# Adding the causal mask of a diagonal score block with VectorE instead of with a matmul, with new planner priorities

## The chip, the core and the metric

The kernel runs on one core of a Trainium2 chip. The core has a matrix engine (TensorE, called PE in the profile; its weight loads are PEld), and three other compute engines: VectorE (DVE), ScalarE (ACT) and GpSimd (POOL). SyncE (SP) issues all the transfers of this kernel. Matmul results land in PSUM, which the kernel divides into eight banks of 128 partitions by 512 fp32 columns. The metric is the device time of one execution in microseconds (us); of several executions the median counts. A separate, profiled execution gives the trace, and its span runs from the first to the last instruction.

## The reference, cut to what matters

The input x is 2048 tokens of 448 numbers. One branch (A) is attention with 16 heads of 28 numbers, in four segments of 512 tokens with a memory carried between segments; the other (B) is a feed-forward layer of width 1792 with SiLU. A learned gate mixes the two.

```python
def _A_ref(x, wq, wk, wv, wo, beta):
    # q, k, v: (x @ w), split into 16 heads of 28 and 4 segments of L = 512
    mask = (ar[:, None] < ar[None, :]) * (-1e9)          # causal, ar = arange(512)
    for s in range(4):
        logits = einsum("bhqd,bhkd->bhqk", qs, ks) * scale + mask
        p = softmax(logits, axis=-1)
        a_dot = einsum("bhqk,bhkd->bhqd", p, vs)
        a_mem = (phi(qs) @ M) / (phi(qs) . z + 1e-6)      # memory of earlier segments
        o = g * a_mem + (1 - g) * a_dot                   # g = sigmoid(beta), per head
        M, z = M + phi(ks)^T vs, z + sum(phi(ks))
    return concat(o) @ wo

b = silu(x @ w1) @ w2
g = sigmoid((x * gate_w).sum(-1, keepdims=True))
return g * _A_ref(...) + (1 - g) * b
```

The softmax needs, for each query row, the maximum of its masked scores. With large query and key weights these scores are large, and the kernel computes the true row maxima.

## The kernel before, in words

**Stages.** The first stage (`project`) loads x and the weights, projects q, k and v for the four segments, and builds the memory. After it two things run side by side: attention, and the feed-forward layer (`ffn`, `unit`) in two passes, over 10 and then 4 of its 14 blocks of 128 hidden columns. The last stage finishes the second feed-forward pass, multiplies the attention output by wo and writes the result.

**Attention by groups.** Attention runs over 16 groups, each four heads of one segment. Function `attention` calls `maxima` for its group. `maxima` loads the group's q and k into a tile named `ring` (four transfers by SP) and then walks a plan of eleven score tiles, each in one PSUM bank of the ring `sc`, which has three banks. Query block i is 128 query rows, and sees only the first 128(i+1) keys, so the tiles are: block 0 of all four heads in one bank (4 x 128 columns), block 1 of two heads per bank (2 x 256), and blocks 2 and 3 of one head per bank (384 and 512). For every tile TensorE computes the scores (line 666, function `go`), and VectorE takes the row maxima (function `red`) into the tile `mx`.

**The mask.** In blocks 1 to 3, one fused VectorE instruction per head (line 676) adds the mask tile `MK`, a 128 x 512 fp32 tile whose last 128 columns hold the causal triangle, and reduces to the maximum. In block 0 the mask comes from TensorE: line 662 multiplies the bf16 identity `identb` by the bf16 triangle `maskb` into all four heads' columns, the four score matmuls accumulate on it, and VectorE reduces once (line 671) over the four heads. The triangle in `maskb` is made once by GpSimd (line 752), from a zeroed tile that the warm-up matmuls of line 740 use first.

**What follows.** When all eleven tiles of a group are reduced, VectorE subtracts a lift (line 684), TensorE transposes the maxima (line 686), ScalarE and VectorE split them in two fp16 parts (lines 688, 690), and SP writes and reloads them as extra rows of `ring`. Then the scores are computed again, transposed (line 1222, also in the `sc` banks), exponentiated by ScalarE (line 1227), masked by GpSimd (lines 1230, 1233), rounded by ScalarE (line 1239), their rest taken by GpSimd (line 1243), and multiplied with v by TensorE (line 1256). Feed-forward products are line 561 (first layer; the same helper does q, k, v and wo) and line 1124 (second layer); their results are worked on by ScalarE (1101, 1105, 1163) and VectorE (1103, 1107).

**What sets the order.** The kernel does not write its instructions in program order. Each step is a task with an engine, an estimated duration, the tasks it needs, the buffers it takes, and a priority (a lower number goes first). The class `Sched` plays the tasks through, always starts the earliest task that can start, and among ready ones takes the lowest priority; on TensorE it adds a price (`PRICE`) for weight loads that would stand uncovered. The result is one fixed order of instructions per engine, and SP's transfers are in one queue. So a change in an estimated duration or a priority can move any instruction of any engine.

**The priorities that the diff touches.** Group t of attention has priority about 40t and head n 10n. `MAXO` is how far ahead of its group the maxima stand. `LOP` is added to the three GpSimd subtractions of a head (line 1243). `FLO` and `FHI` are the ends over which the first feed-forward pass is spread on the same scale, and the second pass and the load of wo start from `FHI`. `WBP` is the priority at which the first ten blocks of w2 are loaded and split (`wb`, lines 521 and 513). `WOP` and `WOT` are how far the wo product and the preparation of its operand (`features`, lines 572, 578, 586) stand ahead of the last additions.

Of the kernel before, what the change touches and what calls it, by code (L numbers as in the profile page):

```python
# [14 lines left out]
OP = mybir.AluOpType  # L15
# [3 lines left out]
S, D, H, DH, NSEG, L, F = 2048, 448, 16, 28, 4, 512, 1792  # L19
# [11 lines left out]
NEG = -1.0e30  # L31
# [10 lines left out]
UP = 2.0 ** 14  # L42
DOWN = 2.0 ** -24
TINY = 2.0 ** -40
WOT = 62.75
TUS = 1.6
TLAT = 4.0

# [3 lines left out]
HO = 0.09  # L52
HS = 0.14
SLACK = 0.88
LOP = 11.31
LATE = 0.08
FIRST = 120.0
WPRIO = 120.0
MAXO = 65.18
FULL = 0.111  # L60
LOCK = 0.06
RB = "cc"
# [15 lines left out]
    return o + VA + VS * k if o or k > VF else -1.0 + 0.1 * k  # L78


PRICE = 31.16
PVRUNS = [((1, 0), 1)]
PVP = 45.12
FLO = -11.7
FHI = 710.96
WOP = 118.93
SZ = 20.35
SZSTEP = 2.77
XPRIO = 74.67
WBP = -20.36  # L90
XLEAD = 146.82


# [149 lines left out]
def infini_mix(ctx: ExitStack, tc: tile.TileContext, x, wq, wk, wv, wo, beta, w1, w2, out):  # L243
    nc = tc.nc
# [39 lines left out]
    def half(cols, n=1):  # L284
        return [(0.0025 + cols * 0.000418, 0.027)] * n

    def pe(seq, fn, *deps, **k):
        t = sch.add("PE", sum(max(a[0], b[1]) for a, b in zip(seq, seq[1:])) + seq[-1][0], fn, deps, **k)
        t.lead, t.tail = seq[0][1], seq[-1][0]
        return t  # L290
# [7 lines left out]
    def dve(cols, fn, *deps, **k):  # L298
        return sch.add("DVE", 0.07 + 0.00104 * cols, fn, deps, **k)
# [4 lines left out]
    def pool(cols, fn, *deps, **k):  # L304
        return sch.add("POOL", 0.1 + 0.0019 * cols, fn, deps, **k)
# [16 lines left out]
    MK = const.tile([128, L], F32, name="mk")  # L322
    identb = const.tile([128, 128], BF, name="identb")
    maskb = const.tile([128, 128], BF, name="maskb")
# [19 lines left out]
    hs = const.tile([128, NSEG], F32, name="hs")  # L344
# [16 lines left out]
    base = ctx.enter_context(tc.tile_pool(name="base", bufs=1))  # L361
# [275 lines left out]
    AT, RS, MKS, ONE, RDONE = {}, {}, [], [], []  # L637
# [4 lines left out]
    def maxima(t, o):  # L642
        rg, mx = Buf(RG), Buf(C["mx"])
        early = o - 70
        rs = []
        for j, scr, st, lo, dup in ((0, qscr[t], QST[t], 0, 2 * DH), (1, kscr[t], KST[t], DH, 0)):
            rs.append(dma(260e3, lambda j=j, lo=lo, scr=scr: start(
                rg.v[lo:lo + 2 * DH, j], scr.rearrange("z d h n -> (z d) h n")), st, *(rs[:1] or RDONE),
                          takes=[] if rs else [rg], uses=[rg], prio=early))
            rs.append(dma(190e3, lambda j=j, dup=dup, scr=scr: start(rg.v[dup:dup + DH, j], scr[0]), st, *rs[:1],  # L650
                          uses=[rg], prio=early))
        RDONE[:] = RS[t] = rs
        reds = []
        plan = [(0, [0, 1, 2, 3]), (1, [0, 1]), (1, [2, 3])] + [(i, [h]) for h in range(4) for i in (2, 3)]
        for q, (i, hs) in enumerate(plan):
            ps = Buf(BK["sc"])
            n = 128 * (i + 1)
            p0 = o - MAXO + 40 * q / len(plan)

            def go(i=i, hs=hs, ps=ps, n=n):  # L660
                if i == 0:
                    nc.tensor.matmul(ps.v, identb, maskb[:, None, :].to_broadcast([128, 4, 128]), start=True,
                                     stop=False, skip_group_check=True)
                for j, hh in enumerate(hs):
                    u = j * n
                    nc.tensor.matmul(ps.v[:, u:u + n], rg.v[:KS, 0, hh, i * 128:(i + 1) * 128], rg.v[:KS, 1, hh, :n],  # L666
                                     start=(i > 0), stop=(i > 0 or j == 3), skip_group_check=(i == 0))

            def red(i=i, hs=hs, ps=ps, n=n):
                if i == 0:  # L670
                    nc.vector.tensor_reduce(mx.v[:, :, 0], ps.v.rearrange("p (h n) -> p h n", h=4), axis=AX.X,
                                            op=OP.max)
                    return
                for j, hh in enumerate(hs):
                    r = ps.v[:, j * n:(j + 1) * n]
                    nc.vector.tensor_tensor_reduce(r, r, MK[:, L - n:], 1.0, NEG, OP.add, OP.max,  # L676
                                                   mx.v[:, hh, i:i + 1])
            m = pe((half(512) if i == 0 else []) + half(n, len(hs)), go, *rs, *MKS, takes=[ps], uses=[rg], prio=p0)
            reds.append(dve(len(hs) * (n + 70) - 70, red, m, *reds[:1], takes=[] if reds else [mx], uses=[ps, mx],
                            prio=p0))  # L680
        pt, mh = Buf(BK["sc"]), Buf(C["mhl2"])
        p0 = o - 20
        s = t // NG
        f0 = dve(100, lambda: nc.vector.tensor_scalar(mx.v, mx.v, lift[:, s:s + 1], None, op0=OP.subtract), *reds, EREADY[s],
                 uses=[mx], prio=p0)
        f1 = pe(half(128), lambda: nc.tensor.transpose(pt.v[:16, :128], mx.v.rearrange("p h i -> p (h i)"), ident), f0,
                takes=[pt], uses=[mx], prio=p0)
        f3 = act(128, lambda: nc.scalar.activation(mh.v[:, 0], pt.v[:16, :128], AF.Copy, scale=1.0 / TALL), f1, takes=[mh],
                 uses=[pt], prio=p0)
        f4 = dve(128, lambda: nc.vector.scalar_tensor_tensor(mh.v[:, 1], pt.v[:16, :128], 1.0 / TALL, mh.v[:, 0],  # L690
                                                             op0=OP.mult, op1=OP.subtract), f3, uses=[pt, mh], prio=p0)
        d1 = dma(16e3, lambda: start(mscr[t].rearrange("z h i n -> (h i) z n"), mh.v), f4, uses=[mh], prio=p0)
        dm = dma(16e3, lambda: start(rg.v[KS:KS + 2, 0], mscr[t].rearrange("z h i n -> z h (i n)")), d1, uses=[rg],
                 prio=p0)
        return rg, rs, dm

    def project():
# [32 lines left out]
        def c1():  # L730
            for v in vtiles:
# [8 lines left out]
        t_wb = pe(half(L, WARM), lambda: [nc.tensor.matmul(  # L740
            wb.v, maskb, maskb[:, None, :].to_broadcast([128, 4, 128]), start=True, stop=True) for _ in range(WARM)],
            t_wm, takes=[wb], prio=-200)
        END1.append(t_wb)
        t_on = dve(32, lambda: nc.vector.memset(ones, -TALL), prio=-50)
        t_mb = dve(128, lambda: nc.vector.tensor_copy(identb, ident), t_id, prio=-50)
# [3 lines left out]
        t_mz = dve(L, lambda: nc.vector.memset(MK, 0.0), prio=-50)  # L749
        MKS.append(pool(128, lambda: nc.gpsimd.affine_select(MK[:, 384:], MK[:, 384:], [[-1, 128]], OP.is_ge, NEG,  # L750
                                                             base=0, channel_multiplier=1), t_mz, prio=-50))
        MKS.append(pool(128, lambda: nc.gpsimd.affine_select(maskb, maskb, [[-1, 128]], OP.is_ge, NEG, base=0,
                                                             channel_multiplier=1), t_wb, t_mb, prio=-50))
        ONE.append(dma(16e3, lambda: start(onescr.rearrange("a h (b n) -> (a h b) n", b=16), ones[:, :32]), t_on,
                       prio=50))

# [286 lines left out]
        for i, (j, src, n, how) in enumerate(pieces):  # L1043
            r, p = Buf(RAW), SZ + i * SZSTEP
# [238 lines left out]
    for t in range(NT):  # L1283
        attention(t)
    prio = spread(FLO, FHI, NSEG * len(PASSES[0]) * (11 * L + TB * 3 * D))
    ends = ffn(0, prio, part)
# [125 lines left out]
```

## Time and profile before

| what | value |
|---|---|
| median of the runs | 568.44 us (567.11 to 569.01, 3 runs) |
| profiled execution, its time | 570.06 us |
| profiled execution, its span | 568.3 us |
| granted TensorE clock, mean | 0.996 |
| PE busy | 549.6 us, 97% of the span |
| DVE busy | 421.8 us, 74% |
| ACT busy | 400.8 us, 71% |
| POOL busy | 360.0 us, 63% |

The page of the profile gives the busy time of each engine, the span in 40 slices, the chain of work that ended last, and the costliest groups of instructions. A group row reads: line, engine, operation, output from input, shape, count, then busy time, mean time of one instruction in ns, and how long the engine stood idle just before those instructions and what ended that idle time. Matmuls are pipelined: a row's mean is the time from a matmul's start to its result, while the next matmul starts earlier, so for TensorE the step from one start to the next in the timeline is what one more matmul takes. Neighbouring VectorE instructions also overlap a little. The profiled execution's time is 1.76 us longer than its span and 1.62 us longer than the median of the runs.

### The profile page before, as it was taken

The page shows a single profiled execution, that of the slowest core. Times are in us where ns is not written, and L with a number is a line of the kernel's source. Part 1 is how long each engine was busy: PE and PEld are TensorE (multiplying, and loading weights), DVE is VectorE, ACT ScalarE, POOL GpSimd, SP SyncE. Part 2 cuts the span into 40 slices and gives each one's busy share as a digit, 9 for nine tenths or more (in the row PEclk, how much of TensorE's full clock was granted, in tenths as well). Part 3 has the DMA queues.
Part 4 walks back from the last instruction along what each step waited for, and adds up shares of the span by engine and source line. Part 5 has one row for each costly group of instructions (what it writes and reads, how often), then busy time and mean ns, then how long its engine had stood idle before and what let it go on. Part 6 is the DMA issues. An engine that isn't in the chain of part 4 may idle for free.

```text
span 568.3 us, 11664 instructions
## 1 busy us (share of the span) xinstructions
PE 549.6 (97%) x4055; PEld 344.0 (61%) x4055; DVE 421.8 (74%) x1096; ACT 400.8 (71%) x695; POOL 360.0 (63%) x502
## 2 busy tenths in 40 slices
PE   8799999999989999999999999999999999999997
PEld 5588878888834455555665554555555555454544
DVE  6999889787868978598865789775888128735644
ACT  6658869675746978889887998877998887213231
POOL 5803347347220688999999988999999993122210
PEclk9999999999989999999999999999999999999999
DMA  8587856534746444422433524374400224798931
GB/s 301 175 249 225 260 150 202 159 108 143 231 147 180 132 152 153 137 72 69 114 101 100 150 78 151 101 157 125 120 14 25 84 67 122 226 232 234 238 104 66
DMA packets 80362, 83.13 MB, mean 146 GB/s; under 512 B 44296, under 2 KB 67976, under 8 KB 80304
## 3 DMA queue, kind: packets, MB, share of 16 engines
q1 hardware_dynamic: 80304, 82.39, 49.8%
q8 instruction: 32, 0.52, 0.4%
q14 instruction: 26, 0.21, 0.1%
HBM read 52.60 MB, written 26.09 MB: 138 GB/s over the span
## 4 chain that ended last, share of the span: by engine, by line
PE 66%; DVE 15%; ACT 8%; DMA 6%; issue 3%; POOL 1%; SPq 1%; DVEq 0%; ACTq 0%; POOLq 0%
PE mm L561 23%; PE mm L1124 18%; PE sc L561 9%; PE sc L1222 4%; DVE sc L676 4%; PE cc L1256 4%; PE sc L666 4%; ACT pf L1227 2%; ACT phl L1239 2%; DVE sizes L385 2%; DVE ghl L1107 1%; DMA rwo<-in_wo_dram 1%; DMA rawf<-in_x_dram 1%; DMA rawf<-in_w_dram 1%; DMA xraw<-in_x_dram 1%
## 5 line engine op out<-in xcount | busy, mean ns | idle before, releaser
L1243 POOL TENSOR_TENSOR phl<-pf,phl 128x384 f16<-128x384 f32 (+1 forms) x192 | 190.1, 1008 | 14.6 <-ACT phl L1239 14.3
L1124 PE MATMUL mm<-wb,ghl 128*128 128x448 f16 (+1 forms) x684 | 146.9, 349 | 0.3 <-DVE ghl L1107 0.3
L561 PE MATMUL mm<-xh,wa 128*128 128x512 f16 x572 | 143.7, 382 | 1.4 <-DVE ghl L1107 1.4
L676 DVE CUSTOM_DVE_ANT_0 sc<-sc,mk 128x384 f32<-128x384 f32 (+1 forms) x192 | 105.0, 570 | 30.1 <-PE sc L666 25.0
L1227 ACT ACTIVATE pf<-sc,es 128x512 f32<-128x512 f32 (+1 forms) x192 | 110.2, 621 | 17.2 <-PE sc L1222 14.1
L1124 PEld LDWEIGHTS <-ghl 128*128 128x128 f16 x684 | 65.1, 97 | 52.7 <-issue 2.1
L561 PEld LDWEIGHTS <-wa 128*128 128x128 f16 x572 | 54.5, 98 | 58.7 <-issue 6.5
L1239 ACT ACTIVATE phl<-pf 128x1280 f16<-128x1280 f32 x64 | 81.3, 1274 | 10.9 <-POOL pf L1233 10.8
L1222 PE MATMUL sc<-ring 86*128 86x512 f16 (+3 forms) x256 | 58.9, 299 | 3.4 <-DVE mx L676 1.5
L666 PE MATMUL sc<-ring 84*128 84x128 f16 (+3 forms) x256 | 57.3, 299 | 1.0 <-DVE mx L676 0.9
L1101 ACT ACTIVATE th<-mm,ths 128x512 f32<-128x512 f32 x52 | 36.1, 697 | 24.3 <-PE mm L561 24.0
L1256 PEld LDWEIGHTS <-phl 128*128 128x128 f16 x1280 | 41.7, 96 | 10.4 <-POOL phl L1243 0.6
L561 PE MATMUL mm<-xT,wqs 128*128 128x512 f32 x176 | 47.1, 404 | 0.0
L572 POOL TENSOR_TENSOR ol<-ol,ml 128x448 f32<-128x448 f32 x12 | 13.8, 1152 | 51.6 <-DMA ol<-o_scr 41.9
L561 PE MATMUL mm<-xT,wks 128*128 128x512 f32 x176 | 45.6, 397 | 0.0
L1103 DVE SCALAR_TENSOR_TENSOR mm<-th,mm 128x512 f32<-128x512 f32 x52 | 35.7, 692 | 11.8 <-ACT th L1101 11.6
L1256 PE MATMUL cc<-vg,phl 128*128 128x29 f16 (+1 forms) x1280 | 43.8, 182 | 0.1
L561 PE MATMUL sc<-wvs,xT 128*128 128x450 f32 x176 | 40.3, 375 | 1.2 <-DVE wvs L819 0.6
L1264 DVE TENSOR_REDUCE oraw<-cc 128x116 f32<-128x232 f32 x64 | 25.2, 393 | 21.5 <-PE cc L1256 21.3
L1107 DVE SCALAR_TENSOR_TENSOR ghl<-mm,ghl 128x512 f16<-128x512 f32 x52 | 35.3, 682 | 6.3 <-ACT ghl L1105 6.2
L1105 ACT ACTIVATE ghl<-mm 128x512 f16<-128x512 f32 x52 | 31.0, 604 | 12.2 <-DVE mm L1103 12.0
L1222 PEld LDWEIGHTS <-ring 86*128 86x128 f16 x256 | 24.0, 97 | 23.3 <-issue 2.9
(167 smaller groups left out, 910.4 us busy)
## 6 DMA issues: line engine op xcount, KB each, us to landing
rawf<-in_w_dram SPq DMA_DIRECT2D x26, 256.0 KB
rawf<-in_w_dram SPq DMA_DIRECT2D x28, 224.0 KB
xraw<-in_x_dram SPq DMA_DIRECT2D x16, 256.0 KB
rawf<-in_x_dram SPq DMA_DIRECT2D x16, 256.0 KB
v_scr<-vt SPq DMA_DIRECT2D x16, 232.0 KB
vg<-v_scr SPq DMA_DIRECT2D x16, 232.0 KB
q_scr<-stg SPq DMA_DIRECT2D x16, 224.0 KB
k_scr<-stg SPq DMA_DIRECT2D x16, 224.0 KB
```

What stands on the lines that cost most here:

```text
L561: nc.tensor.matmul(ps(), *p[i], start=(i == 0), stop=(i == n - 1))
L666: nc.tensor.matmul(ps.v[:, u:u + n], rg.v[:KS, 0, hh, i * 128:(i + 1) * 128], rg.v[:KS, 1, hh, :n], start=(i > 0), stop=(i > 0 or j == 3), ...
L676: nc.vector.tensor_tensor_reduce(r, r, MK[:, L - n:], 1.0, NEG, OP.add, OP.max, mx.v[:, hh, i:i + 1])
L1101: e1 = sact(L, lambda ps=ps, th=th: nc.scalar.activation(th.v, ps.v, AF.Tanh, scale=ths[:, s:s + 1]), m, takes=[th], uses=[ps], prio=p0)
L1103: e2 = dve(L, lambda ps=ps, th=th: nc.vector.scalar_tensor_tensor(ps.v, th.v, 1.0, ps.v, op0=OP.add, op1=OP.mult), e1, uses=[ps, th], prio=p0)
L1107: e4 = dve(L, lambda ps=ps, g=g: nc.vector.scalar_tensor_tensor(g.v[:, 1], ps.v, DOWN, g.v[:, 0], op0=OP.mult, op1=OP.subtract), e3, uses= ...
L1124: nc.tensor.matmul(ps.v[:, lo:hi], g.v[:, y, sl], w.v[:, z, lo:hi], start=(j == 0 and i == 0), stop=(j == len(fs) - 1 and i == 2))
L1222: nc.tensor.matmul(ps.v[:, e:e + w], rg.v[:KK, 1, hh, j * 128:(j + 1) * 128], rg.v[:KK, 0, hh, j * 128:], start=True, stop=True)
L1227: ex.append(sact(e, lambda b=b, ps=ps, pf=pf, e=e: nc.scalar.activation(pf.v[:, b, :e], ps.v[:, :e], AF.Exp, scale=es[:, s:s + 1]), m, *ex ...
L1239: hi = copy(1280, lambda hl=hl, flat=flat: nc.scalar.activation(hl.v[:, 0], flat(), AF.Copy), *mk, takes=[hl], uses=[pf], prio=p0 + 2)
L1243: low = pool(w - u, lambda hl=hl, flat=flat, u=u, w=w: nc.gpsimd.tensor_sub(hl.v[:, 1, u:w], flat()[:, u:w], hl.v[:, 0, u:w]), low, uses=[ ...
L1256: nc.tensor.matmul(p[:, i, :2 - z], hl.v[:, z, u:u + 128], vg.v[:, j, hh, :2 - z], start=(z == zs[0] and i == 0), stop=(z == zs[-1] and j ...
```

## The change

In block 0 the mask matmul goes: the four score matmuls each start and end their own sum, and VectorE adds the last 128 columns of `MK`, repeated for the four heads, to the bank in place before it reduces. `maskb` stays zero and serves only the warm-up. The planner is told 512 columns less for the TensorE task and 430 more for the VectorE task. Eight priority numbers and prices are different.

```diff
-WOT = 62.75
+WOT = 82.89
-LOP = 11.31
+LOP = 14.2
-MAXO = 65.18
+MAXO = 63.68
-PRICE = 31.16
+PRICE = 36.46
-FLO = -11.7
-FHI = 710.96
-WOP = 118.93
+FLO = -10.69
+FHI = 694.58
+WOP = 121.06
-WBP = -20.36
+WBP = -28.66
...
             def go(i=i, hs=hs, ps=ps, n=n):
-                if i == 0:
-                    nc.tensor.matmul(ps.v, identb, maskb[:, None, :].to_broadcast([128, 4, 128]), start=True,
-                                     stop=False, skip_group_check=True)
                 for j, hh in enumerate(hs):
                     u = j * n
                     nc.tensor.matmul(ps.v[:, u:u + n], rg.v[:KS, 0, hh, i * 128:(i + 1) * 128], rg.v[:KS, 1, hh, :n],
-                                     start=(i > 0), stop=(i > 0 or j == 3), skip_group_check=(i == 0))
+                                     start=True, stop=True)
 
             def red(i=i, hs=hs, ps=ps, n=n):
                 if i == 0:
+                    nc.vector.tensor_add(ps.v.rearrange("p (h n) -> p h n", h=4), ps.v.rearrange("p (h n) -> p h n", h=4),
+                                         MK[:, None, L - 128:].to_broadcast([128, 4, 128]))
                     nc.vector.tensor_reduce(mx.v[:, :, 0], ps.v.rearrange("p (h n) -> p h n", h=4), axis=AX.X,
                                             op=OP.max)
                     return
...
-            m = pe((half(512) if i == 0 else []) + half(n, len(hs)), go, *rs, *MKS, takes=[ps], uses=[rg], prio=p0)
-            reds.append(dve(len(hs) * (n + 70) - 70, red, m, *reds[:1], takes=[] if reds else [mx], uses=[ps, mx],
+            m = pe(half(n, len(hs)), go, *rs, *MKS, takes=[ps], uses=[rg], prio=p0)
+            reds.append(dve(len(hs) * (n + 70) - 70 + (430 if i == 0 else 0), red, m, *reds[:1], takes=[] if reds else [mx], uses=[ps, mx],
                             prio=p0))
...
-        MKS.append(pool(128, lambda: nc.gpsimd.affine_select(maskb, maskb, [[-1, 128]], OP.is_ge, NEG, base=0,
-                                                             channel_multiplier=1), t_wb, t_mb, prio=-50))
```

## The prediction

> **What bounds the kernel now.** I read the page's busy times first, then the table by stretches of time over the part where the changed instructions run, then TensorE's timeline there, TensorE's waits, and last the chain of work that ended last.
>
> ```profile
> PE 549.6 (97%) x4055; PEld 344.0 (61%) x4055; DVE 421.8 (74%) x1096; ACT 400.8 (71%) x695; POOL 360.0 (63%) x502
> 240.00:300.00 60.00, 58.60 (x587) 34.37 (x586) 49.03 (x135) 52.75 (x84) 56.21 (x77) 1.00 0.31 88
> 300.00:360.00 60.00, 58.31 (x543) 33.14 (x542) 48.00 (x141) 50.83 (x82) 55.68 (x77) 1.00 0.39 114
> 360.00:440.00 80.00, 79.31 (x750) 45.45 (x748) 61.70 (x175) 68.17 (x109) 75.45 (x105) 1.00 0.37 93
> 176.00:440.00 264.00, 257.80 (x2369) 146.87 (x2367) 210.56 (x590) 224.66 (x357) 231.89 (x316) 1.00 0.39 109
> ```
>
> The stretches list, after the length, the busy time of PE, PEld, DVE, ACT and POOL, then the granted clock. TensorE is busy 97 to 99% of each stretch at full clock, GpSimd 93 to 94%, VectorE 77 to 82%. From 176 to 440 us, where 15 of the 16 mask matmuls run, TensorE stands idle for 264 - 257.8 = 6.2 us and VectorE for 264 - 210.6 = 53.4 us. TensorE leads, GpSimd is close behind it, and VectorE has room on average.
>
> Busy time can flatter TensorE, since overlapping matmuls are counted to their modelled ends. The timeline around the last mask matmul, with the start of each piece in the first column, settles whether it streams:
>
> ```profile
> 422.30 0.38 PE L666 MATMUL sc<-ring 84*128 84x512 f16 x1
> 422.52 0.60 PE L561 MATMUL mm<-xh,wa 128*128 128x512 f16 x2
> 422.95 0.38 PE L662 MATMUL sc<-maskb,identb 128*128 128x512 bf16 x1
> 423.17 0.39 PE L666 MATMUL sc<-ring 84*128 84x128 f16 x4
> 423.39 0.69 PE L1256 MATMUL cc<-vg,phl 128*128 128x29 f16 x20
> 423.91 0.81 PE L561 MATMUL mm<-xh,wa 128*128 128x512 f16 x3
> ```
>
> A 512-column matmul is followed by the next start after 0.22 us (422.30 to 422.52; two take 0.43, 422.52 to 422.95), and the mask matmul follows the same step: 422.95 to 423.17. There is no hole from 422.30 to 423.91 us. Here TensorE is the bound, and a matmul taken out moves everything behind it forward.
>
> The Trainium skill, page "Perfetto Trace Analysis", section "Identifying the Most-Contended Engine", speaks against this reading: it calls matmul busy time no good measure, and wants the load of weights looked at instead. That is 61% here, which by the rule leaves headroom, and then the removed matmuls would only widen gaps and give nothing; the back-to-back starts above disagree for this stretch, so I give that reading a small chance as the second rival below.
>
> **The mask matmul, removed.** The groups of instructions that matter:
>
> ```profile
> L662 PE MATMUL sc<-maskb,identb 128*128 128x512 bf16 x16 | 6.1, 379 | 0.0
> L671 DVE TENSOR_REDUCE mx<-sc 128x4 f32<-128x512 f32 x16 | 11.0, 687 | 3.7 <-PE sc L666 3.6
> L1103 DVE SCALAR_TENSOR_TENSOR mm<-th,mm 128x512 f32<-128x512 f32 x52 | 35.7, 692 | 11.8 <-ACT th L1101 11.6
> L662 PEld LDWEIGHTS <-identb x16: 95/96/98, 64.8 to 422.7; 128*128 128x128 bf16 x16
> ```
>
> Sixteen matmuls go. Their 6.1 us busy holds the overlapping tails; the stream is occupied 16 x 0.215 us (between the 0.21 and 0.22 of the starts) = 3.4 us. Their sixteen weight loads, 16 x 0.096 = 1.5 us, run beside other matmuls and count for nothing: the six pieces above follow without a hole although each has loads of its own. If that cover were gone, it would be 1.5 us more gain. So TensorE gets 3.4 us back, 15/16 of it in the full stage. The four score matmuls keep their shape.
>
> **The add, put in.** The nearest row is line 1103: VectorE, two tensor operands of which one in PSUM, 128x512 fp32 back into PSUM, 0.692 us. The add has that form, so 16 x 0.69 = 11.0 us more busy time. Neighbours overlap, as the starts show:
>
> ```profile
> 247.75 0.69 DVE L671 TENSOR_REDUCE mx<-sc 128x4 f32<-128x512 f32 x1
> 248.36 0.69 DVE L1103 SCALAR_TENSOR_TENSOR mm<-th,mm 128x512 f32<-128x512 f32 x1
> 248.95 0.43 DVE L676 CUSTOM_DVE_ANT_0 sc<-sc,mk 128x256 f32<-128x256 f32 x1
> ```
>
> The step from start to start is 0.59 to 0.61 us, 9.8 us for sixteen; the reduction behind the add needs its result, and I take the full 0.69 for that. VectorE goes from 210.6 to 220.9 busy in the 264 us (15 adds), 84%. Queued behind each add on VectorE are the reduction, the feed-forward steps of lines 1103 and 1107, and the next tiles of line 676; the TensorE work that waits for them is the next score tile, since the bank is held 0.7 us longer, and the second layer.
>
> What of the 11.0 us reaches TensorE? The waits of TensorE in this stretch, and the chain of the whole run and of 176 to 240 us:
>
> ```profile
> PE sc L1222 <- DVE mx L676: 1.5, 6, 0.5
> PE mm L561 <- DVE ghl L1107: 1.4, 4, 0.7
> PE sc L1222 <- ACT pf L1227: 1.0, 3, 0.5
> PE sc L666 <- DVE mx L676: 0.9, 2, 0.6
> PE sc L1222 <- DVE mx L671: 0.5, 1, 0.5
> PE mm L1124 <- DVE ghl L1107: 0.3, 1, 0.3
> ...
> PE 66%; DVE 15%; ACT 8%; DMA 6%; issue 3%; POOL 1%; SPq 1%; DVEq 0%; ACTq 0%; POOLq 0%
> ...
> by line: PE mm L1124 22.2%; DVE sc L676 18.5%; DVE wb L513 8.3%; issue 8.1%; PE sc L1222 5.4%; DVE ghl L1107 5.2%; PE mm L561 4.4%; DVE mx L676 4.0%; PE sc L666 4.0%; DVE mx L684 2.8%; PE cc L1256 2.4%; ACT pf L1227 2.4%; DVE mm L1103 2.1%;
> ```
>
> The lower bound is from the waits: VectorE ends 1.5 + 1.4 + 0.9 + 0.5 + 0.3 = 4.6 us of TensorE's idle time, against 210.6 us of its work, 2.2%; of 11.0 us that is 0.2 us. The upper one is from the chain: VectorE holds 15% of the span, 85 us, of its 421.8 busy, 20%; of 11.0 us that is 2.2 us. I take the middle, 1.2 us. It lies nearer the waits' side than the ceiling of all 11.0 because VectorE itself mostly waits for TensorE at this place:
>
> ```profile
> DVE sc L676 <- PE sc L666: 24.6, 34, 2.4
> ```
>
> It stood 24.6 us in 176 to 440 waiting for score tiles, more than twice what is added.
>
> **GpSimd's select of the mask tile, removed.** One instruction of 0.29 us near the start:
>
> ```profile
> 5.81 0.29 POOL L752 TENSOR_SCALAR_AFFINE_SELECT maskb<-maskb 128x128 bf16<-128x128 bf16 x1 [0.45 <-PE mm L740]
> ```
>
> GpSimd waited 0.45 us for the warm-up matmuls before it, and the work behind it on GpSimd can move up by 0.74 us at most. The page's chain starts with a transfer of x and VectorE's work, and gives GpSimd 1%. I count 0, with 0 and 0.7 us as bounds. `MK`, which the add reads, is made by the select in front of this one on GpSimd, so before 5.8 us, and its first use comes after 64.8 us, when the first mask matmul's weights are loaded: no new wait there.
>
> **The priorities.** No row prices an order that has not been run. Three moves can be bounded, one at a time.
> The first ten w2 blocks are asked for 8.3 units earlier; the chain above gives their VectorE rest (L513 on wb) 8.3% of 64 us, 5.3 us. At best those leave the chain, at worst they come before score tiles and cost the 20% of their time.
>
> ```profile
> L513 DVE SCALAR_TENSOR_TENSOR wb<-rawf,up,wb x14: 666/679/1522, 179.5 to 476.7; 128x448 f16<-128x448 f32 x14
> SPq L319 <- DVE wb L513: 21.2, 10, 5.7
> ```
>
> That is 10 x 0.68 x 0.2 = 1.4 us. SP's queue waits 21.2 us for these steps to free their load buffers, and whatever is issued behind those loads (the q and k of the next group among it) moves with them.
> `FHI` brings the feed-forward forward against attention by 16 units. A group is 40 units, and lasts about (470.2 - 188.1)/16 = 17.6 us by GpSimd's first and last subtraction, so this is 7.2 us of order: more feed-forward early, less left at the end, attention later by some of that.
>
> ```profile
> L1243 POOL TENSOR_TENSOR phl<-pf,phl x192: 902/918/1536, 188.1 to 470.2; 128x384 f16<-128x384 f32 x128, 128x512 f16<-128x512 f32 x64
> L561 PE MATMUL sc<-wos,oT x176: 349/352/353, 486.6 to 556.9; 128*128 128x448 f16 x176
> L586 SPq DMA_TRANSPOSE oT<-oh x16: 1221/1222/1361, 366.2 to 548.2; - x16
> PE cc L415 <- DVE most L411: 2.3, 2, 2.0
> ```
>
> TensorE's wo products fill the end from 486.6 us, and of the 15 rows of its waits in the whole run (the longest shown here, the shortest is line 1124's 0.3 us above) none names `oT`: `WOT` moves the three steps of `features` and SP's transposes earlier for nothing. Were a product to wait for one, a transpose's issue alone is 1.2 us. `LOP` keeps a head's subtractions (10n + 14.2) behind the next head's selects (10n + 10) and ahead of those after (10n + 20), as 11.31 did. `MAXO` puts the maxima 1.5 units, 0.7 us, later. `PRICE`, `WOP` and `FLO` change by little of what they are.
> For their sum I take 0. The upper gain is TensorE's idle time between 24 and 488 us: from the whole table of stretches 1.0 + 0.6 + 2.3 + 1.1 + 1.4 + 1.4 + 1.7 + 0.7 + 0.5 = 10.7 us, of which I let half, 5 us, go; an order can lose as much as it can win, and 5 us is the other end. The table's remaining rows:
>
> ```profile
> 24.00:60.00 36.00, 35.00 (x191) 28.95 (x190) 34.30 (x105) 27.85 (x62) 9.87 (x12) 1.00 0.76 225
> 60.00:130.00 70.00, 69.38 (x402) 58.80 (x401) 58.78 (x159) 53.23 (x122) 35.88 (x57) 1.00 0.57 167
> 130.00:160.00 30.00, 27.73 (x143) 23.59 (x142) 23.05 (x49) 18.55 (x35) 14.98 (x23) 1.00 0.65 199
> 160.00:190.00 30.00, 28.94 (x137) 13.51 (x137) 25.30 (x65) 17.77 (x29) 5.55 (x8) 0.94 0.57 168
> 190.00:240.00 50.00, 48.64 (x429) 27.70 (x427) 38.22 (x106) 42.15 (x68) 41.35 (x57) 1.00 0.47 141
> 440.00:488.00 48.00, 47.49 (x405) 26.14 (x403) 21.39 (x40) 36.60 (x57) 33.91 (x45) 1.00 0.37 120
> ```
>
> **The sum.** -3.4 + 1.2 + 0 + 0 = -2.2 us. The profiled execution took 570.06 us (span 568.3 and 1.76 around it), so 567.9; it lies 1.62 us above the median of 568.44, so a median of 566.2 us, 0.4% faster. A measurement of this kernel tells about 0.3%, 1.7 us, from no change, so this is just outside. With the part of the add between 0.2 and 2.2 it is 565.2 to 567.2.
>
> **The rivals.**
> *GpSimd sets the pace (no gain).* It is 94% busy from 240 to 440 us and its work is untouched, so the attention would end where it did and TensorE's 3.4 us would become waiting, unless feed-forward work fills it; then also the add costs nothing. For it: 56.2 of 60 us. Against it: TensorE is at 58.6 in the same stretch and the end from 488 us is pure TensorE, which any feed-forward done earlier shortens. Time: 568.4 us.
> *VectorE becomes the bound (slower).* Place: 176 to 240 us, where VectorE's lines make up 41% of the chain (18.5 + 8.3 + 5.2 + 4.0 + 2.8 + 2.1), with VectorE busy about 80%, so half of its work is on the chain. If that held for all groups, half of 11.0 us, 5.5, would reach the end: 5.5 - 3.4 = +2.1, 570.5 us. It decides once more than 3.4/11.0 = 31% of the added time reaches TensorE. Against it: from 360 to 440 us VectorE hardly waits on anything TensorE needs, and the 24.6 us above.
> *The new order loses.* Earlier feed-forward takes the banks and ScalarE from attention, or earlier w2 splits delay the first groups: -2.2 + 5 = +2.8, 571.2 us.
> *The new order wins.* The w2 splits leave the chain: -2.2 - 5 = -7.2, 561.2 us.
>
> **How the numbers follow.** My forecast 0.45, GpSimd's pace 0.15, VectorE as the bound 0.17, an order that loses 0.15, one that wins 0.08. Faster by over 0.3% are the winning order and 0.40 of the forecast; the forecast's other 0.05, 0.12 of GpSimd's case and 0.03 of VectorE's are within 0.3%; the rest is slower: 0.48, 0.20, 0.32. The point is 566.2 us. The range takes in all but the outer ends: from 562.0 us, most of the winning order's 5 us, to 573.0 us, where VectorE's 2.1 and part of a losing order's 5 us meet. The forecast's own range is 564.5 to 567.5.
>
> **What would show it.** Right: the 16 rows of line 662 are gone, the add costs 0.66 to 0.72 us each, VectorE gains about 11 us busy, TensorE's busy time falls by 3 to 6 us, and VectorE's part in TensorE's waits from 176 to 440 us stays under 7 us. Wrong: an add of 1 us or more, waits for lines 671, 676 or 1107 that grow by over 3 us, a last GpSimd subtraction later than 470 us by over 3 us, or a TensorE idle sum between 24 and 488 us that moves by more than 5 us, which would be the priorities' doing.

## The result, and the profile after

The changed kernel took 574.11 us (median; 573.39 to 577.11, 4 runs), against 568.61 us (567.11 to 569.01, 4 runs) for the kernel before: a ratio of 1.0099, interval 1.0072 to 1.0126. It is about 5.5 us slower. The prediction was 566.2 us, with a range of 562 to 573.

The profiled execution of the changed kernel took 577.11 us, with a span of 575.3 us, 7.0 us more than the span before. It is the slowest of the four executions, 3.0 us above their median, so that some 1.5 us of the 7.0 belong to the executions that were profiled and not to the change. Line numbers are smaller by one to three from here on: the score matmul is 663, the add 668, the block-0 reduction 670, the fused mask and maximum 675, the feed-forward steps 1102 and 1104, the scores computed again 1219, GpSimd's subtraction 1240.

The busy times on the page of the changed kernel:

```profile
PE 550.0 (96%) x4039; PEld 342.7 (60%) x4039; DVE 433.1 (75%) x1115; ACT 401.4 (70%) x695; POOL 358.6 (62%) x496
```

TensorE has sixteen matmuls less (4055 to 4039), and its busy time is no shorter: 549.6 before, 550.0 now. So all 7.0 us of span, and what the matmuls should have given, are idle time or matmuls that took longer. VectorE has 433.1 - 421.8 = 11.3 us more, as foreseen. The two groups that the change speaks of:

```profile
L668 DVE TENSOR_TENSOR sc<-sc,mk x16: 673/693/700, 66.5 to 431.0; 128x512 f32<-128x512 f32 x16
L1240 POOL TENSOR_TENSOR phl<-pf,phl x192: 906/917/2302, 188.6 to 479.3; 128x384 f16<-128x384 f32 x128, 128x512 f16<-128x512 f32 x64
```

The numbers behind the count are the shortest, median and longest in ns, and then the first start and the last end. The add costs 0.693 us, the 0.69 that was taken for it. GpSimd's last subtraction ends at 479.3 us instead of 470.2. The table by stretches shows where that came from; the first fence is the kernel before, the second the changed one (columns as in the prediction):

```profile
24.00:488.00 464.00, 453.40 (x3571) 291.63 (x3571) 359.77 (x970) 367.90 (x640) 328.87 (x455) 1.00 0.47 136
488.00:570.00 82.00, 76.54 (x406) 39.57 (x405) 42.61 (x76) 17.52 (x28) 13.85 (x12) 0.98 0.63 168
```

```profile
24.00:488.00 464.00, 447.90 (x3526) 287.51 (x3526) 365.93 (x982) 364.91 (x635) 327.50 (x449) 0.99 0.45 130
160.00:190.00 30.00, 27.47 (x118) 11.88 (x116) 24.70 (x65) 16.91 (x28) 4.42 (x8) 0.89 0.64 179
190.00:240.00 50.00, 46.55 (x427) 26.88 (x426) 40.49 (x105) 40.81 (x66) 42.54 (x57) 1.00 0.43 121
176.00:440.00 264.00, 251.26 (x2290) 141.56 (x2288) 213.98 (x590) 219.45 (x347) 223.35 (x302) 0.99 0.40 109
488.00:577.00 89.00, 82.78 (x440) 42.70 (x437) 48.50 (x83) 22.02 (x35) 15.40 (x13) 0.98 0.68 189
```

From 24 to 488 us TensorE stands idle for 464 - 447.9 = 16.1 us, before for 10.6: 5.5 us more. What it did not get done there is left for the end, where it has 82.8 us of work after 488 us instead of 76.5, 6.2 us more. GpSimd, at 223.4 of 264 us, is further from being full than before (231.9). TensorE's waits from 176 to 440 us in the changed kernel (engine, line, what ended the wait: us in all, times, longest):

```profile
PE sc L1219 <- DVE mx L675: 4.3, 12, 0.7
PE sc L663 <- DVE mx L675: 3.2, 4, 1.3
PE mm L561 <- DVE ghl L1104: 1.6, 5, 0.6
PE sc L1219 <- DVE mx L670: 1.4, 1, 1.4
PE sc L1219 <- ACT pf L1224: 1.3, 2, 0.9
PE mm L1121 <- DVE ghl L1104: 0.3, 1, 0.3
```

VectorE ends 4.3 + 3.2 + 1.6 + 1.4 + 0.3 = 10.8 us of them, where it ended 4.6 before. And VectorE's own main wait in the same stretch is as long as it was (24.6 before):

```profile
DVE sc L675 <- PE sc L663: 24.8, 27, 2.9
```

So, set against the kernel before, the added 11 us did not shorten the time in which VectorE waits for score tiles: the two engines wait for each other in turn. But the order of the instructions differs too. In the order of after without any mask work (e7, see the experiments) the rows are:

```profile
PE sc L1219 <- DVE mx L675: 3.2, 8, 0.8
PE sc L663 <- DVE mx L675: 2.3, 4, 1.1
PE mm L561 <- DVE ghl L1104: 1.6, 5, 0.6
PE mm L1121 <- DVE ghl L1104: 0.3, 1, 0.3
DVE sc L675 <- PE sc L663: 29.5, 34, 3.1
```

There VectorE ends 7.4 us of TensorE's waits and itself waits 29.5 us. So in one and the same order the add took 4.7 us out of VectorE's wait and put 3.4 us into TensorE's.

A further part of the 7.0 us is the clock. Shortly before GpSimd's first subtraction (188.6 us), TensorE ran at half clock for some 7 us:

```profile
178.00:179.00 1.00, 0.43 (x2) 0.10 (x1) 1.00 (x5) 0.69 (x1) 0.00 (x0) 1.00 0.69 158
179.00:180.00 1.00, 0.29 (x1) 0.10 (x1) 0.97 (x5) 0.13 (x1) 0.00 (x0) 1.00 0.77 212
180.00:181.00 1.00, 0.54 (x3) 0.19 (x2) 1.00 (x5) 0.54 (x1) 0.00 (x0) 1.00 0.82 294
181.00:182.00 1.00, 0.63 (x3) 0.19 (x2) 1.00 (x5) 0.38 (x1) 0.00 (x0) 0.83 0.67 254
182.00:188.00 6.00, 5.96 (x15) 2.18 (x15) 5.31 (x12) 3.69 (x7) 0.84 (x2) 0.50 0.60 163
188.00:189.00 1.00, 1.00 (x6) 0.50 (x5) 0.00 (x0) 1.00 (x3) 0.40 (x1) 0.76 0.69 208
```

That loses 0.17 + 6 x 0.50 + 0.24 = 3.4 us. The kernel before has one such spell too, half as long:

```profile
160.00:161.00 1.00, 1.00 (x9) 0.79 (x9) 0.07 (x1) 0.00 (x0) 0.90 (x1) 0.85 0.44 135
161.00:164.00 3.00, 3.00 (x9) 1.08 (x8) 2.54 (x12) 0.00 (x0) 1.35 (x3) 0.50 0.27 79
164.00:165.00 1.00, 1.00 (x6) 0.44 (x5) 0.96 (x7) 0.14 (x1) 0.11 (x1) 0.94 0.00 0
```

0.15 + 3 x 0.50 + 0.06 = 1.7 us. So in these two executions about 1.7 of the 7.0 us are clock. Nothing shows this part to be an effect of the change: e19, which runs the instructions of the changed kernel in the same order, has a spell at the same place that loses 1.7 us, and e8, which runs those of the kernel before in the same order, has none there. TensorE's idle time over the whole span is 575.3 - 550.0 = 25.3 us instead of 18.7, 6.6 us more; the matmuls taken out work against both (busy time counts overlapping tails, so the parts do not close to the tenth).

### The profile page after: what moved, and what is told of

Its sections match the earlier page's. It is cut to its first block, busy times and chain, and to the rows that moved or that the text cites. A ratio compares the mean times of both kernels' runs of the same rounds, so it can differ in the third digit from the quotient of the medians.

```text
span 575.3 us, 11644 instructions
## 1 busy us (share of the span) xinstructions
PE 550.0 (96%) x4039; PEld 342.7 (60%) x4039; DVE 433.1 (75%) x1115; ACT 401.4 (70%) x695; POOL 358.6 (62%) x496
## 5 line engine op out<-in xcount | busy, mean ns | idle before, releaser
L1219 PE MATMUL sc<-ring 86*128 86x512 f16 (+3 forms) x256 | 60.5, 300 | 8.0 <-DVE mx L675 4.3
L663 PE MATMUL sc<-ring 84*128 84x128 f16 (+3 forms) x256 | 58.6, 302 | 3.3 <-DVE mx L675 3.2
L1253 PEld LDWEIGHTS <-phl 128*128 128x128 f16 x1280 | 42.0, 96 | 11.3 <-issue 1.6
L1227 POOL TENSOR_SCALAR_AFFINE_SELECT pf<-pf 128x128 f32<-128x128 f32 x64 | 20.1, 314 | 29.6 <-ACT pf L1224 29.4
```

The lines of the kernel that those rows point to most:

```text
L1219: nc.tensor.matmul(ps.v[:, e:e + w], rg.v[:KK, 1, hh, j * 128:(j + 1) * 128], rg.v[:KK, 0, hh, j * 128:], start=True, stop=True)
L1253: nc.tensor.matmul(p[:, i, :2 - z], hl.v[:, z, u:u + 128], vg.v[:, j, hh, :2 - z], start=(z == zs[0] and i == 0), stop=(z == zs[-1] and j ...
```

## The experiments

Three theories stood against each other: that VectorE's added time itself lies on the path; that the score bank, held 0.7 us longer, is what hurts; and that the new order, not the add, loses the time. All ratios are to the kernel before on the same chip, with 95% intervals.

| kernel | median us | ratio | interval |
|---|---|---|---|
| e5: no mask in block 0, order of before | 566.03 | 0.9950 | 0.9917 to 0.9983 |
| e6: matmul and add, order of before | 578.44 | 1.0155 | 1.0125 to 1.0186 |
| e1: add, order of before | 578.75 | 1.0167 | 1.0130 to 1.0204 |
| e7: no mask in block 0, order of after | 570.22 | 1.0028 | 1.0001 to 1.0055 |
| e4: matmul, order of after | 572.92 | 1.0072 | 1.0049 to 1.0096 |
| the change: add, order of after | 574.11 | 1.0099 | 1.0072 to 1.0126 |
| e2: the change with the old priorities | 576.98 | 1.0145 | 1.0107 to 1.0184 |
| e3: before with the new priorities | 582.83 | 1.0233 | 1.0192 to 1.0274 |
| e8: before, `MAXO` 65.0 | 568.83 | 0.9992 | 0.9966 to 1.0017 |
| e15: before, `FHI` 694.58 | 572.71 | 1.0063 | 1.0041 to 1.0084 |
| e16: before, `WBP` -28.66 | 569.47 | 0.9998 | 0.9968 to 1.0028 |
| e19: the change, `FHI` 710.96 | 573.92 | 1.0110 | 1.0069 to 1.0151 |
| e9: before, idle VectorE operation behind the reduction | 575.25 | 1.0111 | 1.0078 to 1.0144 |
| e12: the same in front of the reduction | 574.16 | 1.0118 | 1.0085 to 1.0151 |
| e10: add into SBUF, order of before | 575.69 | 1.0124 | 1.0073 to 1.0176 |
| e11: add into SBUF, order of after | 574.18 | 1.0096 | 1.0061 to 1.0130 |
| e14: before, idle operation at another place | 573.52 | 1.0086 | 1.0055 to 1.0117 |
| e17: add in groups 5 and 6 only | 572.62 | 1.0051 | 1.0028 to 1.0074 |
| e18: add in the other fourteen | 575.52 | 1.0119 | 1.0090 to 1.0147 |

### The parts one at a time, in both orders (e5, e6, e1, e7, e4)

In e1, e5 and e6 the planner's durations and priorities stay those of before, so every instruction that stays keeps its place in its engine's order. Where the matmul is left out, the four score matmuls each start and end their own sum. e5 and e7 reduce block 0 without its mask; e4 also has GpSimd's select of `maskb` again.

```diff
 e5, e1 (order of before)        e6 keeps these
-                if i == 0:
-                    nc.tensor.matmul(ps.v, identb, maskb..., start=True, stop=False, ...)
 e1, e6
+                    nc.vector.tensor_add(ps.v..., ps.v..., MK[:, None, L - 128:]...)
 e7 (order of after)             e4 puts the matmul in its place
-                    nc.vector.tensor_add(ps.v..., ps.v..., MK[:, None, L - 128:]...)
```

> The order of the kernel before, with the mask matmul left out and nothing in its place, so block 0 is reduced without its mask and the output is not the reference's. TensorE-is-the-bound theory: 16 matmuls of 0.215 us less, 565.0 us. Theory that VectorE or GpSimd set the pace, or that the order absorbs it: 568 us. If taking work out of a fixed order lets TensorE fall idle elsewhere (clock), above 568 us.

> The order of the kernel before, mask matmul kept, the add put in as well (the mask is added twice, which changes no maximum). It prices the add alone. Prediction's middle: 568.4 + 1.2 = 569.6 us. The first run of the add in this order was 578.75; if the matmul's 3.4 us are a real gain beside it, this one is 582 us, if they are not, 579 us.

> The instructions of the change (the add on VectorE, no mask matmul) in the order of the kernel before: the planner is told the old costs and priorities, so every queue keeps its order. If the add itself costs the time (VectorE theory), this run shows most of the 5.5 us: 572 to 575 us. If the new order costs it (order theory), this run gives what the prediction's first terms say, 565 to 568 us.

> The order of the changed kernel without add and without mask matmul (block 0 is reduced without its mask; the output is not the reference's). With the run of the mask matmul in this order (572.9) it prices the matmul, with the changed kernel (574.1) the add. TensorE-is-the-bound theory: 572.9 - 3.4 = 569.5 us. If the order alone sets the time: 572 to 574 us.

> The mask matmul instead of the add, in the order of the changed kernel: every queue keeps that order, the planner is told the new costs; GpSimd makes the mask tile right behind the other one. Order theory: the 574 us stay, plus up to 3.4 us of matmuls and less up to 2.2 us of add, 573 to 577 us. VectorE theory: it falls back to 568 to 570 us.

Taking the matmul out gives 0.50%, 2.8 us (e5). The add, put in beside the matmul, costs 1.55%, 8.8 us (e6), and without the matmul 1.67 + 0.50 = 2.17%, 12.3 us (e1 against e5): all of its 11 us of VectorE time, within the uncertainty. In the order of after it costs 0.99 - 0.28 = 0.71%, 4.0 us (the change against e7), and the matmul 0.44%, 2.5 us (e4 against e7). The new order without any mask work is slower than the old one by 0.28 + 0.50 = 0.78%, 4.4 us, yet with the add it is faster by 1.67 - 0.99 = 0.68%, 3.9 us. Each of these differences is uncertain by 0.4 to 0.5%, 2 to 3 us.

The busy rows of the pages of e5, e1 and e7 (spans 566.1, 577.3 and 570.1 us), a fence for each in this order, say in which form the add's time arrives:

```profile
PE 546.7 (97%) x4039; PEld 342.5 (61%) x4039; DVE 418.9 (74%) x1096; ACT 399.5 (71%) x695; POOL 359.2 (63%) x502
```

```profile
PE 554.3 (96%) x4039; PEld 343.6 (60%) x4039; DVE 433.0 (75%) x1112; ACT 403.3 (70%) x695; POOL 361.1 (63%) x502
```

```profile
PE 549.5 (96%) x4039; PEld 343.3 (60%) x4039; DVE 420.2 (74%) x1099; ACT 400.2 (70%) x695; POOL 356.1 (62%) x496
```

From e5 to e1 the span grows by 11.2 us; TensorE is busy 7.6 us longer with the same 4039 matmuls, and idle 3.6 us longer. From e7 to the change the span grows by 5.2 us, of which 0.5 us is busy time and 4.7 us idle. In e1 much of the cost thus comes as slower matmuls: it has three spells at half clock, about 6.8 us lost, and e5 has one, 1.7 us. That is no rule of the old order. One of e1's spells, at 18 to 22 us, comes before the first add. And the page of e6, which has the add in the same order and takes as long (span 577.2 us), reads:

```profile
PE 553.2 (96%) x4055; PEld 343.2 (59%) x4055; DVE 435.2 (75%) x1112; ACT 403.1 (70%) x695; POOL 361.4 (63%) x502
```

Its one spell loses 1.7 us, as in the kernel before; TensorE is busy 3.6 us longer than there and idle 5.3 us longer. So the form in which the cost shows differs between these two kernels, and the cost hardly does.

### The priorities (e2, e3, e8, e15, e16, e19)

```diff
 e2: open kernel is the changed one, all eight numbers as before
 e3: open kernel is the one before, all eight numbers as after
 e8:  -MAXO = 65.18      e15: -FHI = 710.96     e16: -WBP = -20.36     e19 (changed kernel): -FHI = 694.58
 e8:  +MAXO = 65.0       e15: +FHI = 694.58     e16: +WBP = -28.66     e19 (changed kernel): +FHI = 710.96
```

> The changed kernel with its new costs, but the eight priorities of the kernel before, so the planner draws a third order. Priorities theory: 565 to 569 us. VectorE theory: 572 to 575 us. If any order that was not picked for its time loses some us, 570 to 574 us.

> The kernel before, mask matmul and old costs, with the eight new priorities. Priorities theory: 572 to 576 us, since the old instructions cannot help. VectorE theory: 567 to 570 us.

> The kernel before with one priority moved by a trifle: the maxima stand 65.0 instead of 65.18 units ahead of their group, a hundredth of a group. If the old order is one good draw out of a scatter (selection theory), this loses some us, 571 to 580 us. If only the large moves of the eight priorities cost time, it stays at 567 to 570 us.

> The kernel before with FHI alone at its new value (the feed-forward 16 units earlier). With all eight new priorities this kernel takes 582.8 us. If FHI carries that: 575 to 583 us. If no single one does: 567 to 572 us.

> The kernel before with WBP alone at its new value (the first w2 blocks 8 units earlier). If it carries the 14 us of the eight together: 575 to 583 us. If no single one does: 567 to 572 us. The prediction bounded it by -5.3 and +1.4 us: 563 to 570 us.

> The changed kernel with FHI alone back at 710.96. In the kernel before, the new FHI alone cost 3.6 us. If that loss is there in the changed kernel too: 570 to 572 us. If the eight new priorities belong together: 574 to 578 us.

What the new priorities do depends on the durations that the planner is told. In the kernel with the matmul they cost 2.33%, 13 us, where the planner is told the old durations (e3), and 0.72%, 4.1 us, where it is told those of the add (e4). With the add they give 574.1 us, and the old ones 577.0 (e2; the intervals overlap). e1, e2 and e3 came out above every range that was expected of them.

Little can be said of single numbers. In e8 and e19 the traces show the same instructions in the same order on every engine as in the kernel that they start from, so each measures that kernel once more and says nothing of `MAXO`, or of `FHI` in the changed kernel. In e16 one load of w2 and one of w1, with the steps that split them, change places, and that does nothing. `FHI` alone moves much of the order of the kernel before and costs 3.6 us; why was not followed up. The other five were not tried alone. So whether one number carries the order's part stays open.

### The bank or VectorE's time (e9, e12, e10, e11)

e9 and e12 keep the mask matmul and add one VectorE operation per group that touches no score bank, behind the reduction or in front of it (there the bank is held longer). e10 and e11 add into a bf16 SBUF tile and reduce from it, so that the bank is free after the add.

```diff
 e9, e12
+                    nc.vector.tensor_reduce(dum, MK..., axis=AX.X, op=OP.max)   # result unused
 e10, e11
-                    nc.vector.tensor_add(ps.v..., ps.v..., MK...)
-                    nc.vector.tensor_reduce(mx.v[:, :, 0], ps.v..., axis=AX.X, op=OP.max)
+                    nc.vector.tensor_add(msk..., ps.v..., MK...)
+                    nc.vector.tensor_reduce(mx.v[:, :, 0], msk..., axis=AX.X, op=OP.max)
```

> The kernel before in its own order, mask matmul kept, and behind each block-0 reduction one VectorE instruction of about 0.68 us that touches no PSUM bank (a reduction of the mask tile that nobody reads). VectorE gets the time of the add, the bank is given back as early as before. Bank theory (the score bank held longer makes TensorE wait): 568 to 571 us. VectorE-time theory (every delay of VectorE's queue reaches TensorE): 576 to 579 us, like the run with matmul and add (578.4).

> The same instruction in front of the reduction instead of behind it, so that the bank is held 0.6 us longer, as with the add. Both theories: 576 to 579 us. If it stays at 568 to 571 us as well, neither the bank nor VectorE's time is the cause, but the add's traffic on PSUM.

> The change's instructions in the order of the kernel before, but the add writes its result to a bf16 tile in SBUF and the reduction reads that, so the bank is free after the add, as early as after the reduction of the kernel before. Bank theory: the matmul's 3.2 us gained and little lost, 565.5 to 569 us. VectorE-time theory: 575 to 579 us.

> The changed kernel, in its own order, with the add into SBUF. Bank theory: near the run without any mask in this order, 570 to 572 us. VectorE-time theory: 573.5 to 575 us, no change.

Sixteen operations that nobody needs cost 6.3 us (e9), and with the bank held longer 6.7 us (e12): the same. Freeing the bank early gives nothing in the order of after (1.0096 against 1.0099) and nothing certain in the order of before (1.0124 against 1.0167, overlapping). The bank theory falls as the main cause. A share of it stays open: the real add beside the matmul (e6, 1.0155) is above e12 (1.0118), within the uncertainty.

How 0.6 us of VectorE becomes more can be followed in e9. In the kernel before, VectorE hardly pauses between 248 and 264 us (third busy number, 14.53 of 16):

```profile
248.00:264.00 16.00, 14.60 (x143) 8.01 (x142) 14.53 (x40) 14.22 (x25) 14.29 (x19) 1.00 0.31 92
```

```profile
260.04 0.75 DVE L513 SCALAR_TENSOR_TENSOR xh<-rawf,up,xh 64x512 f16<-64x512 f32 x1
260.34 2.35 POOL L1243 TENSOR_TENSOR phl<-pf,phl 128x384 f16<-128x384 f32 x2 [0.91 <-ACT phl L1239]
260.82 0.69 DVE L1107 SCALAR_TENSOR_TENSOR ghl<-mm,ghl 128x512 f16<-128x512 f32 x1
```

The same place in the timeline of e9, first the extra operation, then what stands some 12 us behind it:

```profile
248.83 0.68 DVE L672 TENSOR_REDUCE dum<-mk 128x4 f32<-128x512 f32 x1
...
261.11 1.48 DVE L513 SCALAR_TENSOR_TENSOR xh<-rawf,up,xh 64x512 f16<-64x512 f32 x1
261.13 2.47 POOL L1243 TENSOR_TENSOR phl<-pf,phl 128x384 f16<-128x384 f32 x2 [1.11 <-ACT phl L1239]
262.62 0.69 DVE L1107 SCALAR_TENSOR_TENSOR ghl<-mm,ghl 128x512 f16<-128x512 f32 x1
263.36 1.44 PE L561 MATMUL mm<-xh,wa 128*128 128x512 f16 x3 [1.31 <-DVE ghl L1107]
```

VectorE's line 513 starts 1.07 us later, and now only 0.02 us ahead of GpSimd's line 1243 instead of 0.30. It takes 1.48 us instead of 0.75. Line 1107 behind it starts 1.80 us late, and TensorE waits 1.31 us for it. Then the clock halves:

```profile
262.30:263.00 0.70, 0.00 (x0) 0.00 (x0) 0.67 (x2) 0.70 (x2) 0.70 (x1) 0.50 0.04 12
263.00:264.00 1.00, 0.64 (x2) 0.26 (x2) 1.00 (x3) 0.15 (x1) 1.00 (x3) 0.50 0.03 8
264.00:268.00 4.00, 4.00 (x12) 1.63 (x11) 1.60 (x5) 2.73 (x5) 2.46 (x5) 0.50 0.00 0
268.00:269.00 1.00, 1.00 (x7) 0.50 (x5) 0.50 (x1) 1.00 (x1) 1.00 (x2) 0.50 0.00 0
```

TensorE's busy time from 264 to 269 us is full, at half speed: the three matmuls of line 561 that start at 263.36 us take 1.44 us, and took 0.81 before. The group whose reduction started 0.5 us late at 248 us is followed by one that starts 4.4 us late.

The same stands in all seven traces of the old order with added VectorE work ahead of this place (e1, e6, e9, e10, e12, e14, e17): line 513 begins 0.02 or 0.03 us ahead of GpSimd's line 1243 and takes 1.48 us, TensorE then waits 1.31 us, and a spell at half clock follows. In the kernel before, e5, e8 and e18 line 513 begins 0.10 to 0.30 us ahead and takes 0.75 us, and no spell follows.

### Where it costs (e14, e17, e18)

e14 puts e9's operation behind line 1264 for the first head of each group, a step that takes no part in the maxima. e17 and e18 split the change by groups, in the order of before; the groups left out keep the matmul.

```diff
 e14
+                if hh == 0: nc.vector.tensor_reduce(dum, MK..., axis=AX.X, op=OP.max)
 e17 (e18: t not in (5, 6))
-            def go(i=i, hs=hs, ps=ps, n=n):
-                if i == 0:
+            def go(i=i, hs=hs, ps=ps, n=n, add=t in (5, 6)):
+                if i == 0 and not add:
...
+                    if t in (5, 6): nc.vector.tensor_add(ps.v..., ps.v..., MK...)
```

> The kernel before in its own order with the same sixteen idle VectorE instructions, but behind the sum of each group's first head (line 1264) instead of behind the block-0 reduction. If VectorE's time reaches the end from any place: 573 to 577 us. If the place in front of the score tiles is what makes it dear: 568 to 571 us.

> The order of the kernel before; the add takes the matmul's place in groups 5 and 6 only (of 0 to 15), the other fourteen keep the matmul. With the idle VectorE instruction, 4 of the 6 us of delay arose between the reductions of groups 5 and 6, where VectorE runs 13 us without a pause. Place theory (the cost sits where VectorE has no pause): 571 to 573 us. Uniform theory (each add costs its sixteenth of the 10.3 us): 569.5 us.

> The counterpart: the add in all groups but 5 and 6, the matmul there; order of the kernel before. Place theory: 578.5 less 4 us, 573 to 575.5 us. Uniform theory: 577 to 578 us.

At another place the same operation costs 4.9 us (e14, overlapping e9's interval): it is VectorE's time, not the place in the maxima. The two adds of groups 5 and 6, which stand at about 248 and 265 us, cost 0.51%, 2.9 us; an equal share of e1's 1.67% would be 2/16, 0.21% or 1.2 us. The other fourteen cost 1.19%, 6.8 us, or 0.48 us each net of the matmul. The two parts, 0.51 + 1.19 = 1.70%, make up e1's 1.67%. The trace of e17 has line 513 at its double length again, with a spell behind it that loses 1.7 us:

```profile
260.50 1.48 DVE L513 SCALAR_TENSOR_TENSOR xh<-rawf,up,xh 64x512 f16<-64x512 f32 x1
```

Taken at these medians the pair at 248 to 265 us is dear, and the others cost nearly their own time; an equal share, 0.21%, lies just outside e17's interval. No version that computes the mask was faster than the kernel before by more than its uncertainty.

## Why the prediction was wrong

**The mask matmul, -3.4 us: right.** Measured -2.8 us in the old order and -2.5 in the new one. The reading of the steps from start to start holds.

**The add, its size: right.** 0.693 us each and 11.3 us more VectorE time; 0.66 to 0.72 and 11 were said.

**The add, what reaches TensorE, +1.2 us: this step failed.** It measured 4.0 us in the new order (36% of the added time) and 12.3 us in the old one (the whole, within the uncertainty), against bounds of 0.2 and 2.2 us and a ceiling of 11.0. Both bounds were averages over what VectorE does: its share of TensorE's waits, and of the chain. But an added operation is not an average one. Everything behind it in VectorE's fixed order moves with it until the next pause. That VectorE waits 24.6 us for score tiles gave little cover: in the order of after the add took 4.7 us out of that wait (29.5 us in e7, 24.8 with the add), and in the order of before the wait grew (23.1 us in e5, 28.6 in e1). TensorE too waits for VectorE before it gets to the next tile, and longer with the add (10.8 us against 7.4 in e7 and 4.6 before). Nor was the added time a ceiling for every add: the pair at 248 to 265 us costs 2.9 us, net of the matmuls, for 1.4 us of adds, where line 513 takes twice its time and the clock falls behind it.

**The select, 0: not tried by itself.** GpSimd's busy time is 1.4 us lower.

**The priorities, 0 within 5 us: wrong as one number.** The new order costs 4.4 us without the add and saves 3.9 us with it. The sizes are within the 5 us given, but the sign depends on the add, so that the term could not be added to the others. One of the three moves that were bounded, `WBP` with -5.3 and +1.4 us, exchanges only two loads when tried alone in the kernel before, and does nothing (e16). The measured terms, -2.8 + 12.3 - 3.9 or -2.8 + 4.4 + 4.0, add up to +5.6 us because they are steps along one chain of kernels from before to the change; that they meet the measured +5.5 is no further evidence.

**The rivals.** GpSimd did not set the pace: it has more room than before. VectorE as the bound is the rival that came true in kind; its deciding point, 31% of the added time, was passed clearly in the old order, and in the new one by the median alone (36%, uncertain by some 20). Its price, half of 11.0 us, fits the new order (4.0), but 176 to 240 us was not the only place: from 300 to 440 us TensorE was idle for (60 - 57.39) + (80 - 76.70) = 5.9 us, before for 2.4.

```profile
300.00:360.00 60.00, 57.39 (x538) 32.41 (x536) 48.58 (x132) 50.66 (x81) 53.29 (x74) 1.00 0.38 112
360.00:440.00 80.00, 76.70 (x734) 44.05 (x732) 64.76 (x190) 66.94 (x106) 71.38 (x98) 1.00 0.38 97
```

The order that loses, +5 us, is the other part: taken in the sequence matmul, order, add, the order's 4.4 us and the 2.8 us by which the add was priced too low make 7.2 of the 7.9 us between 566.2 and 574.1.

**What would show it.** Of the signs named for wrong, three came: waits for line 676 (now 675) grew from 1.5 + 0.9 to 4.3 + 3.2 us, the last subtraction came 9.1 us later, TensorE's idle sum moved by 5.5 us. The prediction put this last sign down to the priorities, and e6 speaks against that: with the old priorities and order it has 15.8 us of idle time there, 5.2 more than before.

```profile
24.00:488.00 464.00, 448.24 (x3526) 286.19 (x3527) 365.60 (x976) 363.93 (x630) 327.99 (x453) 1.00 0.45 130
```

Of the signs named for right two failed: VectorE's part of the waits was to stay below 7 us and is 10.8, and TensorE's busy time was to fall by 3 to 6 us and did not.

**The rule on the weight loads.** The prediction set against its own reading the rule of the Trainium skill, "Perfetto Trace Analysis", "Identifying the Most-Contended Engine", by which weight loads at 61% leave headroom; it drew from this that the matmuls taken out would give nothing. e5 measures 2.8 us for them, so here the start-to-start steps were the better guide. The prediction promised this reading a chance as its second rival, but none of its four rivals is this reading.

## What to carry to other kernels

Where engines run fixed orders in turn, idle time of one engine is not by itself room for more work on it: here 53 us of idle VectorE time took in 11 us only at a cost of 4 to 12 us. To price an added operation, look at what stands behind it in its queue until the next real pause of that queue, and put a dummy operation at that place into the old kernel to measure it. An order that was planned for one set of durations can be worth something with those only, so the price of an edit and of its order should be measured apart and not added.

## What the runs showed of the hardware

**The clock can halve after short gaps.** In three places a spell at a granted clock of 0.50 came after gaps of TensorE of at most about 1.3 us. In the kernel before, TensorE was busy for 0.11 + 0.38 + 0.25 = 0.74 of the 3 us from 157 us, in pieces, ahead of the spell that begins in the slice from 160 us:

```profile
157.00:158.00 1.00, 0.11 (x1) 0.00 (x0) 0.47 (x2) 0.85 (x2) 0.26 (x1) 1.00 0.69 236
158.00:159.00 1.00, 0.38 (x1) 0.19 (x1) 0.77 (x2) 1.00 (x3) 0.57 (x1) 1.00 0.13 45
159.00:160.00 1.00, 0.25 (x2) 0.25 (x3) 0.00 (x0) 0.57 (x1) 0.92 (x3) 1.00 0.49 127
```

In the changed kernel it was busy for 1.26 of the 3 us from 178 us, with a longest gap of 1.16 us; in e9 the fall comes within a gap of 1.31 us. The spells shown lose 1.7 us, or 3.4, twice that. The Trainium skill, "TensorE: Matmul & The Clock Gate", "Why this matters for your kernels", warns of gaps longer than about 3 us; these traces show the clock fall after shorter ones. Such gaps do not always bring it down. e8, with the instructions and the order of the kernel before, has the same gaps and keeps the full clock behind them:

```profile
157.69 0.38 PE L979 MATMUL cc<-mhl,phq 112*128 112x232 f32 x1 [1.29 <-ACT phq L875]
159.04 0.32 PE L980 MATMUL cc<-mhl,phq 112*128 112x116 f32 x1 [0.97 <-POOL phq L877]
160.00:165.00 5.00, 5.00 (x25) 2.25 (x23) 4.29 (x20) 0.77 (x2) 1.64 (x4) 1.00 0.25 72
```

The changed kernel keeps it too after gaps of 1.36 us at 193.60 and 1.32 us at 198.59 us. That the gaps are what brings the clock down is read from what stands ahead of the spells, and was not tried by itself; what decides when it falls stays open.

**A VectorE operation on SBUF can double beside GpSimd.** Line 513 on 64x512 elements took 0.75 us where it began 0.10 to 0.30 us ahead of GpSimd's line 1243 (four traces), and 1.48 us where it began 0.02 or 0.03 us ahead of it (seven traces). So a shift of a few tenths of a microsecond between two engines can add 0.7 us. What in the start times decides it was not tried.
